# GEMM2's matmuls placed one by one inside the products of GEMM1, for ten of the 24 of a pair

## The chip, the cores and the metric

The kernel runs on one core of one Trainium2 chip. The metric is the device time of the program in microseconds (us), as the median of several runs. A profiled execution of the same program gives the trace that is read below.

## What is computed

Eight batches with eight heads of linear attention feed a feed-forward layer of 4608 tokens, 512 channels and 2048 hidden units:

```python
q_s = exp(q - max(q, -1)); q_s /= sum(q_s, -1) + 1e-9      # over head_dim
k_s = exp(k - max(k, 2));  k_s /= sum(k_s, 2) + 1e-9       # over the sequence
kv  = einsum('bhsd,bhse->bhde', k_s, v)
x   = einsum('bhsd,bhde->bhse', q_s, kv)                   # -> (4608, 512)
h   = x @ w_in                                             # (4608, 2048)  GEMM1
g   = h * clip(h + 3, 0, 6) / 6
out = g @ w_out                                            # (4608, 512)   GEMM2
```

## The kernel before

The 4608 tokens are nine blocks of 512, numbered 0 to 8. Every large operand is held as a high and a low part in a rounded 32-bit type, and every product is three matmuls (high by high, high by low, low by high). Blocks 0 and 1 go through a plain GEMM1 with matmuls that move 512 columns. Blocks 2 to 8 use a seven-product (Strassen-like) form of GEMM1: `fast_pair(j, pair)` handles two of the 16 hidden chunks at once, so there are eight pairs a block and 56 pairs in all.

In a pair, `product(n, ps, name)` is called for n = 0 to 6. Each product is six matmuls that move 256 columns (two halves of the contraction by three part combinations) and accumulates in one of three PSUM tiles: `z` (pool `ps_a`, two buffers, shared with the attention's `pm`, `pkv` and `px`) for product 0, `y` for products 2 and 6, `x` for products 1, 3, 4 and 5 (`x` and `y` in pool `ps_h`, two buffers in all, so each pair gets the same two banks). Between the products ScalarE and VectorE combine the tiles into `first` and `second`, apply the activation (`swish`), and `split` the results into high and low parts: `one` at L545, behind product 5, and `two` at L553 and L554, which wait in the list `rest` and are issued in the next pair. At its end each product calls `fetch(1)`, one DMA on the queue of SyncE that brings a factor of weights (the product twelve calls later) into the ring slot just freed.

GEMM2 of a pair is 24 matmuls that move 512 columns, 12 for `one` and then 12 for `two`, made by the generator `work` and put in the list `pend` when the pair's products are all issued (L1028). `fill(n)` takes the next n out of `pend` and issues them. So the GEMM2 matmuls of a pair are issued during the next pair, in the gaps between products: 4, then 3 and 4, then 3 and 4, then 3 and 3. The four PSUM accumulators `po` of a block are read out by `store` when the last hidden chunk's matmuls for them are done, ScalarE for the even ones and VectorE for the odd, and a DMA writes each to the output. In the last chunk of a block the matmuls come accumulator by accumulator; in the others the four that use the low part come last.

The attention of later blocks is prepared in small steps that `half` puts in `plan`, 64 places to a block and eight to a pair; `tick(j, n)` issues the steps of place n. Some of them are DMAs (`load`, `load_k`), some GpSimd copies (`q_swap`), and four kinds use TensorE: `k_turn` (`pm`), `kv_mm` (`pkv`, 40 small matmuls), and `x_mm` (`px`).

The order on TensorE, VectorE, ScalarE and GpSimd in this part is the program's own; the order of the DMAs on SyncE's queue is left to the scheduler.

The core of the order, in the text's shorthand (256 and 512 are the columns moved), is for one pair before the change:

```text
p0 p1 | 4 x 512 | tick 0 | p2 | tick 1 | p3 | 3 x 512 | tick 2 | 4 x 512 | tick 3
p4 | 3 x 512 | tick 4 | 4 x 512 | tick 5 | p5 | 3 x 512 | tick 6 | 3 x 512 | p6 | tick 7
```

Of the kernel before, what the change touches and what calls it, by code (L numbers as in the profile page):

```python
# [31 lines left out]
def attention_moe(  # L32
# [32 lines left out]
    NB = NT // TB  # L65
    NFC = w.shape[0]
# [17 lines left out]
    def ordered(ins):  # L84
        tc.keep_in_program_order(ins)

    def mm(out, lhsT, rhs, start, stop, goes_on=False):
        ordered(
            nc.tensor.matmul(  # L89
                out, lhsT, rhs, start=start, stop=stop, skip_group_check=goes_on  # L90
            )
        )
# [27 lines left out]
    def split(hi, lo, src, engine=nc.vector):  # L120

        nc.scalar.copy(hi, src)  # L122
        engine.tensor_sub(lo, src, hi.bitcast(F32))  # L123
# [76 lines left out]
    FAST = 2  # L200
# [208 lines left out]
    def factors(j):  # L409

        if j not in spare:
            (x21, x22), (t2, t3) = ((x[:, 0:2], x[:, 2:4]) for x in x_block(j % 2))
            x11, t1, t4 = (wi[3 * (j % 2) + i] for i in range(3))
            t = [x11, x21, x22, t1, t2, t3, t4]
            spare[j] = [
                (y.rearrange("p a b -> p (a b)")).rearrange(
                    "p (e i n) -> p e i n", e=2, i=2
                )
                for y in t
            ]  # L420
        return spare[j]
# [44 lines left out]
    def fetch(count):  # L466
        for _ in range(count):
            key = next(wanted, None)
            if key is None:
                return  # L470
            j, pair, n = key
            f, h = RING[next(turn) % len(RING)]
            t = wi[f].rearrange("p a n -> p (a n)")[:, h * TB : (h + 1) * TB]
            t = t.rearrange("p (e n) -> p e n", e=2)
            nc.sync.dma_start(t.bitcast(F32), kept[pair][:, ORDER[n][0]])
            come[key] = t
# [8 lines left out]
    def fast_pair(j, pair):  # L485

        to = factors(j)
        x = ps_h.tile([P, TB], F32, name="ph", tag="ph")[:, 0:HT]
        y = ps_h.tile([P, TB], F32, name="ph", tag="ph")[:, 0:HT]
        z = ps_a.tile([P, TB], F32, name="pz", tag="pa")[:, 0:HT]  # L490
        seen = set()

        def product(n, ps, name):
            w_hi, w_lo = (come[j, pair, n][:, e] for e in (0, 1))
            f_hi, f_lo = (to[ORDER[n][1]][:, e] for e in (0, 1))
            for i in range(2):
                c = slice(i * P, (i + 1) * P)
                for k, (w, f) in enumerate(((w_hi, f_hi), (w_hi, f_lo), (w_lo, f_hi))):
                    first = name not in seen
                    seen.add(name)  # L500
                    mm(ps, w[:, c], f[:, i], first, i == 1 and k == 2, True)
            del come[j, pair, n]
            fetch(1)

        def swish(r, h):
            nc.scalar.activation(r, h, AF.Relu, bias=three, scale=1.0)  # L506
            nc.vector.scalar_tensor_tensor(r, r, 6.0, h, op0=ALU.min, op1=ALU.mult)  # L507

        first = moe.tile([P, TB], F32, name="first", tag="g_hi", bufs=3)
        second = moe.tile([P, TB], F32, name="second", tag="g_lo", bufs=3)  # L510
        places = [wi[12 + 2 * (pair % 2) + n] for n in (0, 1)]
        one, two = ((t[:, 0], t[:, 1]) for t in places)
        at = 8 * pair
        product(0, z, "z")
        product(1, x, "x")
        nc.scalar.copy(first[:, 0:HT], x)
        if rest:
            rest.pop(0)()
        fill(4)
        tick(j, at)  # L520
        if rest:
            rest.pop(0)()
        product(2, y, "y")
        nc.vector.tensor_add(first[:, 0:HT], first[:, 0:HT], z)
        tick(j, at + 1)
        product(3, x, "x")
        nc.scalar.copy(second[:, 0:HT], x)
        r = moe.tile([P, TB], F32, name="g", bufs=2)
        swish(r[:, 0:HT], first[:, 0:HT])
        fill(3)  # L530
        tick(j, at + 2)
        fill(4)
        tick(j, at + 3)
        product(4, x, "x")
        nc.scalar.copy(second[:, HT:], x)
        nc.vector.tensor_add(second[:, HT:], second[:, HT:], y)
        fill(3)
        tick(j, at + 4)
        fill(4)
        tick(j, at + 5)  # L540
        product(5, x, "x")
        swish(r[:, HT:], x)
        fill(3)
        tick(j, at + 6)
        split(*one, r)  # L545
        fill(3)
        product(6, y, "y")
        nc.vector.tensor_add(second[:, 0:HT], second[:, 0:HT], y)  # L548
        r = moe.tile([P, TB], F32, name="g", bufs=2)
        nc.scalar.activation(r, second, AF.Relu, bias=three, scale=1.0)  # L550
        tick(j, at + 7)
        nc.vector.scalar_tensor_tensor(r, r, 6.0, second, op0=ALU.min, op1=ALU.mult)  # L552
        rest.append(lambda: nc.scalar.copy(two[0], r))  # L553
        rest.append(lambda: nc.vector.tensor_sub(two[1], r, two[0].bitcast(F32)))  # L554
        return [one, two]
# [3 lines left out]
    def tick(j, n):  # L559
        for fn in plan.pop((j, n), ()):  # L560
            fn()
# [322 lines left out]
    def work(j, fs, gs):  # L884

        for f, g in zip(fs, gs):
            for n, (fn, x) in enumerate(gemm2(f, *g, acc(j))):
                yield fn, x, (j, n // 3) if f == NFC - 1 and n % 3 == 2 else None

    def run(got):  # L890
        fn, x, done = got
        fn(*x)
        if done:
            j, t = done
            store(j, t, acc(j)[t])

    def fill(n=10**6):
        while pend and n:
            got = next(pend[0], None)
            if got is None:  # L900
                pend.pop(0)
                continue
            run(got)
            n -= 1
# [82 lines left out]
    def block1():  # L987
        for p in range(NFC // 2 - 1):
            d = fast_weights(p)
            for n in (0, 1, 3, 4, 5, 7):  # L990
                at(1, 8 * (p + 1) + n, lambda d=d: next(d, None))
        d7 = fast_weights(NFC // 2 - 1)
        for n in (0, 1, 3, 4, 5, 8):
            at(2, n, lambda: next(d7, None))
        for j in range(FAST, NB):
            lead = {FAST: 3, FAST + 1: 6}.get(j, 0)
            half(j, 0, 2, lead)
            half(j, 1, 3, 32, 2 if j == FAST else 0)
        fill()
        for f in range(NFC):  # L1000
            g = gemm1(1, f)
            tick(1, 4 * f)
            tick(1, 4 * f + 1)
            g.mms()
            g.relu()
            tick(1, 4 * f + 2)
            g.times()
            g.hi()
            if f % 2 and f >= 11:
                fetch(2 if f < 15 else 12 - len(come))  # L1010
            keep = f == NFC - 1
            if not keep:
                fill(6)
            tick(1, 4 * f + 3)
            gs = g.lo()
            if not keep:
                fill(6)
            pend.append(work(1, [f], [gs]))
# [3 lines left out]
    with tc.manual_schedule(engines=ORDERED):  # L1022
        block1()
        for j in range(FAST, NB):
            for pair in range(NFC // 2):
                gs = fast_pair(j, pair)
                fill()
                pend.append(work(j, [2 * pair, 2 * pair + 1], gs))  # L1028
        while rest:
            rest.pop(0)()  # L1030
        fill()
# [60 lines left out]
```

## Time and profile before

| | |
|---|---|
| median of 3 runs | 865.53 us (865.02 to 866.68) |
| the profiled execution | 865.39 us, of which the span of the instructions is 863.3 us |
| TensorE matmuls busy | 840.3 us, 97% of the span, 5380 instructions |
| weight loads busy (TensorE) | 735.7 us, 85% |
| VectorE busy | 625.1 us, 72% |
| ScalarE busy | 444.1 us, 51% |
| GpSimd busy | 70.7 us, 8% |
| granted TensorE clock | 0.998 of full |

Busy times are shares of the span. A matmul's own record lasts from its start to the modelled end of its pipeline, so records of successive matmuls overlap; the pace is read from start to start. In the rows PE is TensorE's matmuls, PEld its weight loads (each matmul has one, and it runs beside the matmul before it), DVE VectorE, ACT ScalarE, POOL GpSimd, SP SyncE.

### The profile page before, as it was taken

How to read it: one execution, taken by the hardware profiler on the slowest of the kernel's cores; microseconds unless marked ns; L12 is line 12 of the kernel's file. 1: busy time of each engine (PE TensorE's matmuls, PEld its weight loads, DVE VectorE, ACT ScalarE, POOL GpSimd, SP SyncE). 2: the span in 40 equal slices, each digit the busy share in tenths (PEclk: the TensorE clock that was granted, in tenths of full speed). 3: DMA queues.
4: the chain of work that ended last, by engine and by line, in shares of the span. 5: the costliest groups of instructions: out<-in, count | busy, mean ns of one | idle time of the engine just before them, and what ended most of it. 6: DMA issues, size and time to landing. Idle time of an engine off the chain costs nothing.

```text
span 863.3 us, 15152 instructions
## 1 busy us (share of the span) xinstructions
PE 840.3 (97%) x5380; PEld 735.7 (85%) x5380; DVE 625.1 (72%) x1275; ACT 444.1 (51%) x897; POOL 70.7 (8%) x244
## 2 busy tenths in 40 slices
PE   4799999999999999999999999999999999999998
PEld 3587888888889898989898989999898998989996
DVE  6998995989877776777776777676767676664333
ACT  6898773454544454544545445444444544453333
POOL 4000000101020101010000101010101010100000
PEclk9999999999999999999999999999999999999999
DMA  9778542537887668767776777676865666557541
GB/s 368 270 304 273 170 130 75 185 117 226 275 270 257 216 214 259 223 203 231 249 237 199 245 240 251 185 243 201 272 184 167 192 216 195 171 163 226 173 134 49
DMA packets 97114, 182.56 MB, mean 211 GB/s; under 512 B 9744, under 2 KB 24080, under 8 KB 94992
## 3 DMA queue, kind: packets, MB, share of 16 engines
q1 hardware_dynamic: 96192, 180.03, 65.0%
q10 hardware_dynamic: 576, 1.05, 0.4%
q0 software_dynamic: 272, 0.52, 0.3%
q8 instruction: 43, 0.70, 0.3%
q14 instruction: 31, 0.25, 0.1%
HBM read 156.93 MB, written 24.12 MB: 210 GB/s over the span
## 4 chain that ended last, share of the span: by engine, by line
PE 90%; DVE 4%; ACT 2%; DMA 2%; issue 1%; SPq 0%; POOL 0%; ACTq 0%; POOLq 0%; DVEq 0%
PE po L89 44%; PE ph L89 36%; PE pz L89 5%; PE px L89 3%; PE pkv L89 2%; DMA kq<-in_q_dram 1%; DMA w<-v 1%; DVE v L162 1%; ACT raw L168 1%; DVE w L188 0%; DMA raw<-in_w_dram 0%; DVE v L152 0%; DVE v L156 0%; PE pm L95 0%; ACT qt L297 0%
## 5 line engine op out<-in xcount | busy, mean ns | idle before, releaser
L89 PE MATMUL po<-w,w 128*128 128x512 f32 x1008 | 263.3, 395 | 0.0
L89 PEld LDWEIGHTS po<-w,w 128*128 128x128 f32 x1008 | 177.1, 189 | 29.0
L89 PE MATMUL ph<-w,w 128*128 128x256 f32 x1008 | 147.5, 282 | 0.0
L89 PEld LDWEIGHTS ph<-w,w 128*128 128x128 f32 x1008 | 139.7, 191 | 9.1
L89 PE MATMUL ph<-x_lo,w 128*128 128x256 f32 (+1 forms) x800 | 144.8, 301 | 0.4 <-DVE x_lo L123 0.3
L89 PE MATMUL ph<-x_hi,w 128*128 128x256 f32 (+1 forms) x592 | 135.5, 333 | 2.8 <-DVE x_lo L387 2.8
L89 PEld LDWEIGHTS ph<-x_lo,w 128*128 128x128 f32 x800 | 113.7, 189 | 11.7 <-DVE x_lo L123 0.5
L89 PEld LDWEIGHTS ph<-x_hi,w 128*128 128x128 f32 x592 | 96.1, 190 | 18.8 <-DVE x_lo L387 3.6
L621 POOL COPY swap<-qm 32x16 f32<-32x16 f32 x224 | 58.7, 262 | 626.3 <-DVE qm L615 592.3
L89 PE MATMUL po<-w 128*128 128x512 f32 x336 | 88.4, 395 | 0.1
L550 ACT ACTIVATE g<-second,three 128x512 f32<-128x512 f32 x56 | 40.7, 726 | 68.6 <-DVE second L548 67.5
L89 PEld LDWEIGHTS po<-w 128*128 128x128 f32 x336 | 58.9, 189 | 10.3 <-ACT w L553 0.5
L89 PE MATMUL po<-w,g_hi 128*128 128x512 f32 x256 | 67.6, 396 | 0.0
L123 DVE TENSOR_TENSOR w<-g,w 128x512 fp32r<-128x512 f32 x56 | 38.8, 693 | 30.7 <-ACT w L122 29.4
L507 DVE SCALAR_TENSOR_TENSOR g<-g,ph 128x256 f32<-128x256 f32 x56 | 23.5, 420 | 45.2 <-ACT g L506 44.9
L89 PEld LDWEIGHTS po<-w,g_hi 128*128 128x128 f32 x256 | 47.1, 188 | 10.1 <-issue 0.7
L552 DVE SCALAR_TENSOR_TENSOR g<-g,second 128x512 f32<-128x512 f32 x56 | 38.7, 691 | 22.9 <-ACT g L550 22.9
L553 ACT CAST w<-g 128x512 fp32r<-128x512 f32 x56 | 34.9, 623 | 31.7 <-DVE g L552 31.7
L506 ACT ACTIVATE g<-ph,three 128x256 f32<-128x256 f32 x56 | 26.4, 472 | 45.4 <-PE ph L89 45.4
L89 PE MATMUL pz<-x_hi,w 128*128 128x256 f32 x336 | 49.5, 283 | 0.0
L554 DVE TENSOR_TENSOR w<-g,w 128x512 fp32r<-128x512 f32 x56 | 38.8, 692 | 13.9 <-ACT w L553 12.1
L507 DVE SCALAR_TENSOR_TENSOR g<-g,first 128x256 f32<-128x256 f32 x56 | 23.7, 423 | 34.6 <-ACT g L506 34.6
(133 smaller groups left out, 1195.0 us busy)
## 6 DMA issues: line engine op xcount, KB each, us to landing
w<-wf SPq DMA_DIRECT2D x392, 256.0 KB, 3.1
raw<-in_w_dram SPq DMA_DIRECT2D x16, 1024.0 KB, 11.1
out_dram<-ob SPq DMA_DIRECT2D x36, 256.0 KB, 3.4
vt<-in_v_dram SPq DMA_DIRECT2D x28, 325.0 KB, 5.5
wf<-w SPq DMA_DIRECT2D x16, 512.0 KB, 3.8
kt<-in_kT_dram SPq DMA_DIRECT2D x28, 288.0 KB, 3.2
ke<-in_k_dram SPq DMA_DIRECT2D x24, 320.0 KB, 4.3
qt<-in_qf_dram SPq DMA_DIRECT2D x28, 256.0 KB, 3.7
```

What stands on the lines that cost most here:

```text
L89: nc.tensor.matmul(out, lhsT, rhs, start=start, stop=stop, skip_group_check=goes_on)
L123: engine.tensor_sub(lo, src, hi.bitcast(F32))
L162: nc.vector.scalar_tensor_tensor(vu, raw(1), 0xC0000000, vu, op0=ALU.bitwise_and, op1=ALU.bitwise_or)
L168: nc.scalar.activation(low, low, AF.Copy, scale=2.0**-29)
L506: nc.scalar.activation(r, h, AF.Relu, bias=three, scale=1.0)
L507: nc.vector.scalar_tensor_tensor(r, r, 6.0, h, op0=ALU.min, op1=ALU.mult)
L550: nc.scalar.activation(r, second, AF.Relu, bias=three, scale=1.0)
L552: nc.vector.scalar_tensor_tensor(r, r, 6.0, second, op0=ALU.min, op1=ALU.mult)
L553: rest.append(lambda: nc.scalar.copy(two[0], r))
L554: rest.append(lambda: nc.vector.tensor_sub(two[1], r, two[0].bitcast(F32)))
L621: nc.gpsimd.tensor_copy(swaps[hp][r : r + QD], qms[hp][o : o + QD])
```

## The change

Five of the 24 GEMM2 matmuls of a pair go one at a time behind each of the first five matmuls of product 0, and five more in the same way inside product 2. The other 14 go in two runs of seven, between products 3 and 4 and between 4 and 5. There are none between 1 and 2 or between 5 and 6 any more. Since product 0 of a pair comes before that, the five in it are the last five of the pair before the previous one: five stay in `pend` when a pair ends. In the first pair of block 2 and the last pair of block 8 product 0 takes none; so after the last pair 10 older matmuls are left to issue ahead of that pair's own 24.

All eight ticks move: tick 0 is now inside product 0, behind its third matmul, tick 1 is behind product 1, tick 2 behind product 2, and ticks 3 to 6 stand where 4 and 3 matmuls of 512 columns alternate in the other order. The `fill()` that drained `pend` at a pair's end is gone.

```text
p0 with 5 x 512 (tick 0 inside) | p1 | tick 1 | p2 with 5 x 512 | tick 2 | p3 | 4 x 512 | tick 3
3 x 512 | tick 4 | p4 | 4 x 512 | tick 5 | 3 x 512 | tick 6 | p5 | p6 | tick 7
```

```diff
-        def product(n, ps, name):
+        def product(n, ps, name, among=0, at=None):
...
                     mm(ps, w[:, c], f[:, i], first, i == 1 and k == 2, True)
+                    if 3 * i + k < among:
+                        fill(1)
+                    if at is not None and 3 * i + k == 2:
+                        tick(j, at)
...
-        product(0, z, "z")
+        product(0, z, "z", 0 if (j, pair) in ((FAST, 0), (NB - 1, NFC // 2 - 1)) else 5, at)
         product(1, x, "x")
         nc.scalar.copy(first[:, 0:HT], x)
         if rest:
             rest.pop(0)()
-        fill(4)
-        tick(j, at)
+        tick(j, at + 1)
         if rest:
             rest.pop(0)()
-        product(2, y, "y")
+        product(2, y, "y", 5)
         nc.vector.tensor_add(first[:, 0:HT], first[:, 0:HT], z)
-        tick(j, at + 1)
+        tick(j, at + 2)
         product(3, x, "x")
         nc.scalar.copy(second[:, 0:HT], x)
         r = moe.tile([P, TB], F32, name="g", bufs=2)
         swish(r[:, 0:HT], first[:, 0:HT])
-        fill(3)
-        tick(j, at + 2)
         fill(4)
         tick(j, at + 3)
+        fill(3)
+        tick(j, at + 4)
         product(4, x, "x")
         nc.scalar.copy(second[:, HT:], x)
         nc.vector.tensor_add(second[:, HT:], second[:, HT:], y)
-        fill(3)
-        tick(j, at + 4)
         fill(4)
         tick(j, at + 5)
+        fill(3)
+        tick(j, at + 6)
         product(5, x, "x")
         swish(r[:, HT:], x)
-        fill(3)
-        tick(j, at + 6)
         split(*one, r)
-        fill(3)
         product(6, y, "y")
         nc.vector.tensor_add(second[:, 0:HT], second[:, 0:HT], y)
...
             for pair in range(NFC // 2):
                 gs = fast_pair(j, pair)
-                fill()
                 pend.append(work(j, [2 * pair, 2 * pair + 1], gs))
```

## The prediction

> **What bounds the kernel.** I read the page's busy times and its chain of waits first, then the stage that the change touches in stretches, then one pair of it in the order of time.
>
> ```profile
> span 863.3 us, 15152 instructions
> PE 840.3 (97%) x5380; PEld 735.7 (85%) x5380; DVE 625.1 (72%) x1275; ACT 444.1 (51%) x897; POOL 70.7 (8%) x244
> ...
> PE 90%; DVE 4%; ACT 2%; DMA 2%; issue 1%; SPq 0%; POOL 0%; ACTq 0%; POOLq 0%; DVEq 0%
> ```
>
> The chain that ended last is 90% TensorE. In stretches (start and end, length, PE's busy time and instructions, granted clock, DMA share, GB/s), from the first product of block 2 to the last product of block 8, and then the tail:
>
> ```profile
> 224.78:853.40 628.62, 628.26 (x4249) 1.00 0.68 212
> 853.40:863.33 9.93, 6.20 (x26) 0.99 0.27 106
> ```
>
> TensorE leaves 0.36 us of 628.62 uncovered, at clock 1.00. So no engine or transfer holds this stage as a whole; it lasts as long as its matmuls follow each other, and the change can win only in their pace, at waits inside it, or in the tail. One pair of block 8, which has no attention steps, in the order of time (start, length of the group's records, tile, columns moved, count):
>
> ```profile
> 830.21 1.55 PE L89 MATMUL po<-w,w 128*128 128x512 f32 x6
> 831.60 0.88 PE L89 MATMUL ph<-w,w 128*128 128x256 f32 x6
> 832.31 0.88 PE L89 MATMUL pz<-x_hi,w 128*128 128x256 f32 x6
> 833.03 0.88 PE L89 MATMUL ph<-w,w 128*128 128x256 f32 x6
> 833.75 1.09 PE L89 MATMUL po<-w,w 128*128 128x512 f32 x4
> 834.68 1.59 PE L89 MATMUL ph<-x_lo,w 128*128 128x256 f32 x12
> 836.10 1.78 PE L89 MATMUL po<-w,w 128*128 128x512 f32 x7
> 837.72 0.88 PE L89 MATMUL ph<-w,w 128*128 128x256 f32 x6
> 838.43 1.78 PE L89 MATMUL po<-w,w 128*128 128x512 f32 x7
> 840.04 0.88 PE L89 MATMUL ph<-x_hi,w 128*128 128x256 f32 x6
> 840.76 1.32 PE L89 MATMUL po<-w,w 128*128 128x512 f32 x5
> ```
>
> From start to start: the 24 of 512 columns take 1.39 + 0.93 + 1.62 + 1.61 = 5.55 us, the 42 of 256 take 2.15 + 1.42 + 0.71 + 0.72 = 5.00, the pair 10.55. In the middle of a long run a 256 takes 120 ns (832.31 to 833.03 is six). In block 1, where only 512s follow each other, the chain of waits gives their undisturbed pace, 2.72 / 12 = 227 ns:
>
> ```profile
> 204.12 2.72 PE ph L89 x12
> ```
>
> So the pair's 512s pay 5.55 - 24 x 0.2267 = 0.11 us above that. Where it sits shows in single durations, grouped by shape in slits of time (the last number before the idle column is the mean ns): at 837.72 (last 512 of a run, first 256 behind it), 833.76 (last 256s of a run, first 512 behind them) and 833.99 (that first and the second 512).
>
> ```profile
> L89 PE MATMUL po<-w,w 128*128 128x512 f32 x1 | 0.4, 389 | 0.0
> L89 PE MATMUL ph<-w,w 128*128 128x256 f32 x1 | 0.3, 278 | 0.0
> ```
>
> ```profile
> L89 PE MATMUL ph<-w,w 128*128 128x256 f32 x2 | 0.4, 283 | 0.0
> L89 PE MATMUL po<-w,w 128*128 128x512 f32 x1 | 0.4, 396 | 0.0
> ```
>
> ```profile
> L89 PE MATMUL po<-w,w 128*128 128x512 f32 x2 | 0.6, 397 | 0.0
> ```
>
> A 256 behind a 512 is 278 - 283 = 5 ns shorter than its followers, and half of the locked 512 is 113 ns against 120, so I take 114 ns for it, 6 below the run. I read this as its weight load: behind a 512 it has been hidden, behind another 256 it ends a little too late. The first 512 behind a 256 pays 396 - 389 = 7 ns, the next 2 x 397 - 396 - 389 = 9 ns, and by the end of a run nothing.
>
> **The change part by part.**
>
> *Ten single 512s.* No instruction is added or removed; 5 + 5 of the 24 change places. A pair has had four runs of 256s, so four cheap first ones. Now the runs are 13, four singles, 8, four singles, 7 and 6, twelve in all: 8 more at 6 ns, -48 ns. On the other side the two runs of seven cost 1.62 + 1.61 - 14 x 0.2267 = 0.056 us above the locked pace, and the ten singles, each behind a 256, 7 ns: 0.070. Together 0.126 against 0.11 before, +16 ns. Net -32 ns a pair. The trace has no 512 between two 256s, so both ends: at best a single is free on both sides (the 512 at 227, the 256 at 114), 10 x 7 = 70 ns better than that; at worst the 9 ns which a second 512 pays is paid by the 256 that stands in its place, 90 ns worse. I take the values in between since a lone 512 has exactly the neighbours whose rows stand above: a 256 before it (396) and behind it a 256 that follows a 512 (278). 54 pairs have all ten, two have five: 55 x 32 ns = -1.8 us.
>
> A rule speaks against this. The Trainium skill, page "TensorE: Matmul & The Clock Gate", section "LDWEIGHTS (loading the stationary operand)", gives a load of 128 columns as 128 / 1.2, 107 ns, and its section "Back-to-back issue gap" gives 262 cycles at 2.4 GHz, 109 ns, for a 256-column matmul: the load would fit under each 256 already, and a 512 in between would hide nothing. By that this term would be 0, not -1.8 us. The trace has 120 and not 109 ns in the run.
>
> *The tail.* After product 6 of the last pair come 24 of 512 columns:
>
> ```profile
> 853.40 6.28 PE L89 MATMUL po<-w 128*128 128x512 f32 x24
> 856.38 0.69 DVE L554 TENSOR_TENSOR w<-g,w 128x512 fp32r<-128x512 f32 x1 [0.69 <-ACT w L553]
> 856.40 0.30 PEld L89 LDWEIGHTS po<-w 128*128 128x128 f32 x2 [0.51 <-ACT w L553]
> 857.12 2.14 PEld L89 LDWEIGHTS po<-w 128*128 128x128 f32 x10 [0.43 <-DVE w L554]
> ```
>
> From the first start to the last they take 6.28 - 0.39 = 5.89 us, where 23 locked ones take 5.21: 0.68 too long, 0.03 of it the usual start of a run, the rest waits for the high and the low part of `two`. With the change product 6 stands right behind product 5 and 10 older 512s (2.3 us) come first. Product 5 ended at 851.30 (853.40 less product 6 and the six 512s). Counted from there the matmuls of `two` then begin at 0.72 + 2.3 + 2.7 = 5.7 us and need the low part 0.45 later. The high part was ready at 856.4, which is 5.1, the low part at 856.38 + 0.69, which is 5.77, and the chain to them hangs on product 5 (below, bank `y`). No wait is left, with 0.4 us to spare: -0.65 us. If that cover were short, up to the same 0.65 would come back.
>
> *The first pair of block 2.* Product 2 waits there for the factor T3:
>
> ```profile
> 227.14 0.92 PE L89 MATMUL ph<-x_lo,w 128*128 128x256 f32 x4
> 228.40 1.21 PE L89 MATMUL ph<-x_lo,w 128*128 128x256 f32 x8 [0.34 <-DVE x_lo L123]
> ```
>
> T3 comes when it did, and product 2 now gets there 0.93 us earlier, without four 512s ahead of it; but four singles run before its fifth matmul, which is the one that waits for the low part. The same 512s are done by 228.4: 0, at most 0.2 either way.
>
> *Bank `y`.* Product 6 no longer has six 512s ahead of it, so the sum that frees `y` for the next product 2 has less time. In block 8 (product 5 ends at 840.76):
>
> ```profile
> 842.58 0.69 DVE L123 TENSOR_TENSOR w<-g,w 128x512 fp32r<-128x512 f32 x1 [0.69 <-ACT w L122]
> 843.19 0.42 DVE L548 TENSOR_TENSOR second<-second,ph 128x256 f32<-128x256 f32 x1
> ```
>
> It ends 2.85 us after product 5, held by the low part of `one` ahead of it on VectorE, not by product 6. The next product 2 begins 0.72 + (0.72 + 5 x 0.233) + 0.71 = 3.3 us after product 5 (before: 4.47, from 830.21 to 834.68). The cover is 0.45 us; a VectorE later than that stops TensorE for the difference. Pairs with attention steps can be later, by the rows
>
> ```profile
> 438.78 1.55 PE L89 MATMUL po<-w,w 128*128 128x512 f32 x6
> 442.05 0.42 DVE L548 TENSOR_TENSOR second<-second,ph 128x256 f32<-128x256 f32 x1
> ```
>
> that is 3.7 us after product 5, but behind that pair six matmuls of `px` now stand ahead of product 2, which move as many columns as three 512s (by the locked pace an estimated 0.7 us). I cost it at 0.
>
> *The ticks.* All eight move by some 1.3 us or less against TensorE. VectorE's part of a tick now often comes ahead of a sum that waits for TensorE, which fills idle time. `kv_mm` and the first `x_mm` keep 256s on both sides; `k_turn` and the second `x_mm` pass from between 512s to between a 512 and a 256:
>
> ```profile
> 424.28 0.86 PE L89 MATMUL po<-w,w 128*128 128x512 f32 x3
> ...
> 426.01 0.88 PE L89 MATMUL ph<-x_hi,w 128*128 128x256 f32 x6
> ```
>
> ```profile
> 433.31 0.98 PE L89 MATMUL ph<-x_lo,w 128*128 128x256 f32 x6
> 434.12 1.09 PE L89 MATMUL po<-w,w 128*128 128x512 f32 x4
> ```
>
> With `pm` in it a run of seven takes 1.73 us, so it costs 1.73 - 1.62 = 0.11 us; six 256s behind `pkv` cost 0.81 - 0.71 = 0.10, so the neighbour matters by 0.01: 0, with 0.3 for 40 such places.
>
> *Queues and banks.* SyncE still gets one fetch a product, 12 products ahead (by the pair above some 18 us), against 3.1, and for a tick's load 3.2,
>
> ```profile
> w<-wf SPq DMA_DIRECT2D x392, 256.0 KB, 3.1
> kt<-in_kT_dram SPq DMA_DIRECT2D x28, 288.0 KB, 3.2
> ```
>
> us to land, and a tick's loads are read seven ticks or more later, each over 1 us. GpSimd's four copies of a `q_swap` have one tick or more before VectorE reads them; the shortest, from tick 3 to tick 4, now has three 512s in it (0.7 us) instead of those and a product, and a late copy would hold VectorE first. The stores of accumulators 2 and 3 move to product 0 of a block's second pair; their banks are next written some 3 us later, in and behind product 2, against one read-out of 512 columns on ScalarE or VectorE. All 0.
>
> Sum against the profiled execution's own 865.39 us: -1.8 - 0.65 gives 863.0. The median of the runs is 865.53, 0.14 above it, which I do not carry.
>
> **The rivals.**
>
> *Nothing to hide.* Singles cost what their kind costs on average now, and only the tail is won: 865.39 - 0.65 = 864.7. For it: the change's own term is 32 ns of 10.55 us, and the 256s behind the run of four in the pair above go at 1.42 / 12 = 118 ns, so they do not simply swing between 114 and 120. Against it: the 278 and the 396. The Trainium skill's load rule, cited above, gives this time.
>
> *Free on both sides.* With time to spare on every load the singles fall to 227 and 114: 55 x 70 ns more, 863.0 - 3.9 = 859.1. For it: the last 512 of a run has 389. Against: that takes some five 512s to come about.
>
> *The wait is handed on* (slower). After a disturbed 512 the next matmul pays 9 ns whatever its kind, so the 256 costs 123: 863.0 + 550 x 9 ns = 868.0. For it: the second 512's excess cannot be its load, which had a whole 512 to hide under. Against: it fades along the run. It makes the kernel slower from 7.5 ns a single on (867.1).
>
> **How the numbers follow.** Chances: forecast 0.38, nothing to hide 0.28, free 0.16, handed on 0.14, a late `y` or another new wait 0.04. About 0.2% (1.7 us) is what a measurement of this kernel can tell from no change; 863.0 is 2.4 below 865.39, and a quarter of its chance falls within 1.7. Faster: 0.16 + 0.29 = 0.45; same: 0.09 + 0.28 = 0.37; slower 0.18. The forecast's own range is 862.0 to 864.3 (0.3 for ticks, 0.2 for block 2, 0.65 for the tail, 2 ns on each single). The range for 8 in 10 runs from 859.5 to 867.3: it leaves out the handed-on case and a late bank (0.18) and little of the free one.
>
> **What would show it.** In the profile after: a 512 in product 0 or 2 of about 396 ns and the 256 behind it of about 278; a pair of block 8 of 10.52 us; no wait of PE's loads for L553 and L554 behind the last product; no new idle of PE ahead of product 2. Wrong it is if single 256s show 285 or more, if a pair takes 10.6, or if the waits name L548.

## The result, and the profile after

The kernel after the change takes 874.13 us (median of 6 runs, 871.89 to 876.24); the kernel before, on the same chip, 866.11 us (6 runs, 864.77 to 867.91). The ratio is 1.0096, 95% interval 1.0079 to 1.0114: about 1% slower, where 863.0 was forecast and 867.3 was the end of the range.

The profiled execution took 876.14 us. Its page (span; busy time and share of each engine; the chain of waits):

```profile
span 874.0 us, 15156 instructions
PE 848.4 (97%) x5380; PEld 737.4 (84%) x5380; DVE 627.3 (72%) x1275; ACT 444.7 (51%) x897; POOL 74.5 (9%) x244
...
PE 83%; DVE 7%; ACT 2%; DMA 2%; issue 1%; POOL 0%; ACTq 0%; POOLq 0%; DVEq 0%
```

The share of VectorE in the chain rose from 4% to 7%, though its busy time is nearly the same (627.3 against 625.1): it is waited for more often, not busier. In stretches (start and end, length; busy time and instructions of PE, PEld, DVE, ACT and POOL in turn; granted clock, DMA share, GB/s), from the first product of block 2 to the last product of block 8, and the tail:

```profile
226.32:862.51 636.19, 632.68 (x4239) 564.48 (x4238) 425.03 (x923) 297.68 (x625) 52.56 (x192) 1.00 0.68 209
862.51:874.00 11.49, 7.90 (x36) 6.20 (x34) 4.20 (x7) 3.16 (x5) 0.00 (x0) 0.95 0.24 91
```

The first stretch is 636.19 us with ten matmuls fewer (4239 for 4249), where it was 628.62, and TensorE is uncovered for 3.51 us instead of 0.36. The clock is 1.00 as before. The start of block 2 is not compared: in the profiles of all the kernels below it lies anywhere from 222.2 to 227.6 us, ahead of the pairs that were edited (only z1_runs and z2_lead8 also move one step of block 1, by one place). I therefore call *net* the time from the first product of block 2 to the end of the span, against the same of before. It is +9.18 us for the change: +7.57 up to the last product and +1.61 in the tail, to the end of the last instruction at 874.05; the tail has ten more matmuls of 512 columns (2.27 us).

TensorE's waits, by what it waited for (total us, times, longest), among those at least 0.2 us long:

```profile
PE ph L89 <- DVE second L539: 1.9, 5, 0.4
...
PE ph L89 <- DVE second L548: 0.6, 1, 0.6
...
PE px L89 <- DVE v L723: 0.3, 1, 0.3
...
PE ph L89 <- ACT second L538: 0.2, 1, 0.2
```

None of these stood in the same list of before. L548 is the sum `second += y` behind product 6, the name that the prediction gave as a sign that it is wrong. The last pair of block 8 shows it:

```profile
851.54 0.88 PE L89 MATMUL ph<-w,w 128*128 128x256 f32 x6
...
853.36 0.69 DVE L123 TENSOR_TENSOR w<-g,w 128x512 fp32r<-128x512 f32 x1 [0.69 <-ACT w L122]
853.97 0.41 DVE L548 TENSOR_TENSOR second<-second,ph 128x256 f32<-128x256 f32 x1
854.43 0.39 PE L89 MATMUL ph<-x_lo,w 128*128 128x256 f32 x1 [0.57 <-DVE second L548]
```

Product 6 starts at 851.54 and is through 0.72 us later. The sum that reads it starts at 853.97, since VectorE has the low part of `one` (L123) ahead of it, and that waits for ScalarE's cast. Product 2 of the new pair (854.43) needs the bank which the sum frees, and stands still.

A larger loss is in pair 1 of blocks 3 to 6. Pair 1 of block 4 (its product 5 starts at 431.79):

```profile
430.65 1.08 POOL L621 COPY swap<-qm 32x16 f32<-32x16 f32 x4 [9.52 <-DVE qm L615]
430.95 0.35 ACT L538 COPY second<-ph 128x256 f32<-128x256 f32 x1
431.76 0.17 DVE L624 TENSOR_TENSOR qm<-qm,swap 128x16 f32<-128x16 f32 x1 [0.78 <-POOL swap L621]
431.97 0.69 DVE L625 TENSOR_TENSOR qt<-qt,qm 128x512 f32<-128x512 f32 x1
432.58 0.41 DVE L539 TENSOR_TENSOR second<-second,ph 128x256 f32<-128x256 f32 x1
433.05 0.98 PE L89 MATMUL ph<-w,w 128*128 128x256 f32 x6 [0.38 <-DVE second L539]
```

GpSimd's swap keeps VectorE waiting for 0.78 us, a step of the attention follows, and only then comes L539, the sum that frees `y` for product 6. Product 6 starts 1.26 us behind product 5 (431.79 to 433.05) instead of 0.72. And in pair 0 product 2 waits for its factor T3 (pair 0 of block 4):

```profile
413.24 0.41 DVE L548 TENSOR_TENSOR second<-second,ph 128x256 f32<-128x256 f32 x1
413.74 0.72 ACT L550 ACTIVATE g<-second,three 128x512 f32<-128x512 f32 x1 [1.15 <-DVE second L548]
414.37 0.60 ACT L122 CAST x_lo<-v 128x512 fp32r<-128x512 f32 x1
415.01 0.69 DVE L123 TENSOR_TENSOR x_lo<-v,x_lo 128x512 fp32r<-128x512 f32 x1 [1.36 <-ACT x_lo L122]
415.75 0.19 PEld L89 LDWEIGHTS ph<-x_lo,w 128*128 128x128 f32 x1 [0.36 <-DVE x_lo L123]
```

The late sum releases the relu (L550), ScalarE's cast for T3 (L122) stands behind that relu, and T3's low part (L123) behind the cast.

From the first matmul of a pair to that of the next, against the same pair of before (us; the first pair of block 2 and the last of block 8 hold five matmuls of 512 columns fewer, 1.13 us):

| block | pair 0 | 1 | 2 | 3 | 4 | 5 | 6 | 7 |
|---|---|---|---|---|---|---|---|---|
| 2 | -0.69 | +0.12 | +0.27 | +0.01 | +0.56 | +0.70 | 0.00 | +0.13 |
| 4 | +0.22 | +0.67 | 0.00 | +0.10 | +0.29 | +0.07 | 0.00 | +0.11 |
| 8 | +0.21 | +0.04 | +0.04 | +0.04 | +0.04 | +0.04 | +0.04 | -0.30 |

So the loss is +0.04 us in an undisturbed pair, and waits of 0.1 to 0.8 us at certain places.

### The profile page after: what moved, and what is told of

Its sections match the earlier page's. It is cut to its first block, busy times and chain, and to the rows that moved or that the text cites. A ratio compares the mean times of both kernels' runs of the same rounds, so it can differ in the third digit from the quotient of the medians.

```text
span 874.0 us, 15156 instructions
## 1 busy us (share of the span) xinstructions
PE 848.4 (97%) x5380; PEld 737.4 (84%) x5380; DVE 627.3 (72%) x1275; ACT 444.7 (51%) x897; POOL 74.5 (9%) x244
## 4 chain that ended last, share of the span: by engine, by line
PE 83%; DVE 7%; ACT 2%; DMA 2%; issue 1%; POOL 0%; ACTq 0%; POOLq 0%; DVEq 0%
PE po L89 40%; PE ph L89 33%; PE pz L89 4%; PE px L89 3%; PE pkv L89 2%; DMA kt<-in_kT_dram 1%; DMA w<-v 1%; ACT w L122 1%; DVE w L123 1%; ACT g L550 1%; DVE ke L604 0%; DVE qt L625 0%; DVE w L188 0%; DVE v L162 0%; ACT g L510 0%
## 5 line engine op out<-in xcount | busy, mean ns | idle before, releaser
L89 PE MATMUL po<-w,w 128*128 128x512 f32 x1008 | 301.1, 395 | 0.0
L89 PEld LDWEIGHTS po<-w,w 128*128 128x128 f32 x1008 | 184.1, 189 | 33.6
L89 PE MATMUL ph<-x_lo,w 128*128 128x256 f32 (+1 forms) x800 | 187.5, 302 | 1.1 <-DVE second L548 0.6
L89 PEld LDWEIGHTS ph<-x_lo,w 128*128 128x128 f32 x800 | 132.0, 189 | 12.2 <-DVE x_lo L123 2.6
L89 PEld LDWEIGHTS ph<-w,w 128*128 128x128 f32 x1008 | 133.9, 190 | 9.1 <-DVE second L539 3.0
L89 PE MATMUL po<-w 128*128 128x512 f32 x336 | 97.7, 394 | 0.0
L89 PE MATMUL pz<-x_hi,w 128*128 128x256 f32 x336 | 93.1, 282 | 0.0
L550 ACT ACTIVATE g<-second,three 128x512 f32<-128x512 f32 x56 | 40.5, 723 | 64.6 <-DVE second L548 63.5
L123 DVE TENSOR_TENSOR w<-g,w 128x512 fp32r<-128x512 f32 x56 | 38.8, 692 | 38.4 <-ACT w L122 38.4
L89 PEld LDWEIGHTS pz<-x_hi,w 128*128 128x128 f32 x336 | 63.1, 190 | 0.1
L552 DVE SCALAR_TENSOR_TENSOR g<-g,second 128x512 f32<-128x512 f32 x56 | 38.6, 690 | 23.0 <-ACT g L550 23.0
L553 ACT CAST w<-g 128x512 fp32r<-128x512 f32 x56 | 34.8, 622 | 30.5 <-DVE g L552 30.4
L122 ACT CAST w<-g 128x512 fp32r<-128x512 f32 x56 | 34.7, 620 | 27.3 <-DVE g L511 26.8
```

What stands on the lines that cost most here:

```text
L89: nc.tensor.matmul(out, lhsT, rhs, start=start, stop=stop, skip_group_check=goes_on)
```

## The experiments

*The theory* that stands at the end: the singles cost a little, and the rest comes from VectorE. With product 6 directly behind product 5, the sum L548 still has to wait for the low part of `one`, so it and all that follows it in VectorE's queue come later against the products of the next pair. *The rivals*: the singles themselves, a price for each passage from one width to the other, and the moved ticks. "Net" is read from the profile, the ratio from runs of both kernels on one chip; the chips differ from row to row, so medians of different rows are not to be compared.

| kernel | median us | ratio to before (95%) | net us |
|---|---|---|---|
| the change | 874.13 | 1.0096 (1.0079, 1.0114) | +9.18 |
| x1_runs5 | 875.11 | 1.0101 (1.0079, 1.0123) | +7.71 |
| x2_tick4 | 873.74 | 1.0088 (1.0063, 1.0113) | +6.62 |
| x3_three | 870.34 | 1.0053 (1.0033, 1.0073) | +4.73 |
| y1_both | 871.98 | 1.0072 (1.0052, 1.0092) | +5.62 |
| x4_hold | 864.35 | 0.9983 (0.9966, 1.0000) | -0.71 |
| y2_four | 868.02 | 1.0017 (0.9998, 1.0035) | +1.63 |
| y3_thirteen | 868.30 | 1.0032 (1.0012, 1.0053) | +2.72 |
| y5_sumfirst | 866.33 | 1.0011 (0.9992, 1.0030) | +1.00 |
| w1_near | 887.09 | 1.0240 (1.0220, 1.0261) | +20.32 |
| s1_runs5sum | 866.11 | 0.9992 (0.9979, 1.0004) | +0.06 |
| z1_runs | 865.92 | 1.0004 (0.9991, 1.0018) | -0.14 |
| z2_lead8 | 867.04 | 1.0020 (1.0005, 1.0035) | +3.58 |

### x1_runs5: the change without singles

```diff
-        product(0, z, "z", 0 if (j, pair) in (...) else 5, at)
+        product(0, z, "z", 0, at)
+        fill(0 if (j, pair) in (...) else 5)
...
-        product(2, y, "y", 5)
+        fill(5)
+        product(2, y, "y")
```

> The changed kernel with no single 512s: the five of product 0 go in one run between products 0 and 1, the five of product 2 in one run between products 1 and 2; all steps of ScalarE and VectorE and all ticks stay as changed. Theory 'two costs': the 9.2 us lost behind block 1 are some 2.2 us from the singles themselves (54 pairs by 0.04) and some 7 us from new waits on VectorE's order. Then pairs without attention go back from 10.59 to 10.55, the waits of product 2 (for T3 and, in the last pair, for y: 1.1 and 0.7 us) go since product 2 starts 1.2 us later in its pair, and the 0.63 us wait of product 6 in the second pair of blocks 3 to 6 stays: 869 to 871 us. Rival 'the interleaving is all of it': pairs with attention also fall back to the time before, 865 to 866 us.

An undisturbed pair of block 8 goes from +0.04 to +0.01 us, and the last pair loses its wait for `y`, since the five now stand ahead of product 2 (-0.30 to -1.11, that is 0.81 us). Pair 1 of blocks 3 to 6 keeps its +0.67. The ratio isn't better than the change's (875.11 us, where 869 to 871 was expected), though the intervals are wider than the 1.5 us by which the profiles differ. The wait for T3, which was expected to go, went in blocks 7 and 8 (pair 0 at -0.01), but pair 0 of blocks 3, 5 and 6 keeps +0.17 to +0.19. The singles are not where the 9 us went.

### x2_tick4, x3_three, y1_both: a tick back, a run back

```diff
 # x2_tick4, to the change
         fill(3)
-        tick(j, at + 4)
         product(4, x, "x")
         nc.scalar.copy(second[:, HT:], x)
         nc.vector.tensor_add(second[:, HT:], second[:, HT:], y)
+        tick(j, at + 4)
```

```diff
 # x3_three, to the change; y1_both has both edits
         tick(j, at + 5)
-        fill(3)
         tick(j, at + 6)
         product(5, x, "x")
...
+        fill(3)
         product(6, y, "y")
```

> The changed kernel with tick 4 moved back behind product 4 and the sum of second and y (where it stood before), all else as changed. Theory 'the sum behind tick 4': VectorE's steps of tick 4 stand ahead of the sum that frees y for product 6, and it waits there 0.54 us in the second pair of blocks 3 to 6 and the sixth of block 2. Then these waits go: 3 us off, 870.5 to 872 us, the other pairs as they are. Rival 'interleaving': no change, 874 us.

> The changed kernel with the run of three between products 4 and 5 moved to between products 5 and 6; singles as changed. Theory 'product 6 too near to product 5': the chain of VectorE that frees y and makes T3's low part hangs on product 5, so with nothing between 5 and 6 the next product 2 comes 1.2 us too early for it. Then the 0.73 us wait in the last pair, the 0.2 us waits in the first pair of blocks 3 to 8 and the 0.1 us waits of px go: 1.9 to 2.5 us off, 872 us; the 0.54 us waits of product 6 stay. Rival 'interleaving': no change, 874 us.

> The changed kernel with both mends at once: tick 4 behind product 4 and its sum, and the run of three between products 5 and 6 (singles kept). Theory 'two costs': hardly a wait of TensorE is left, pairs without attention stay at 10.59 us (0.04 above before, the price of ten singles), pairs with attention come to within 0.1 of that: the stage 2 to 3 us above before for the same work, the tail 0.65 below: 867 to 868 us. Rival 'other waits take their place' (tick 4 behind product 4 made the pairs with the second x_mm 0.2 us longer when it was moved alone): 869 us or more.

With tick 4 behind the sum L539, pair 1 falls from +0.67 to +0.01 and the waits for L539 are gone from the list. But pairs 3 and 7 rise to +0.29 to +0.41, and the ratio hardly moves: 873.74 us, where 870.5 to 872 was expected. With three 512s between products 5 and 6, pair 0 falls from +0.22 to -0.08 and the last pair from -0.30 to -0.99, as VectorE then has 0.7 us more for what hangs behind product 5; pair 1 stays at +0.59. The first pair of block 2 loses more there, +1.14 instead of +0.44 for the same work (its wait is read further below). The two together were expected to add up, at 867 to 868 us, and did not (871.98): pair 1 is at +0.29, pairs 3 and 7 at +0.27 to +0.39. So the ticks' places decide where TensorE waits, not whether. What both edits leave as it was, beside the singles, is the order of the sum and the low part on VectorE; y5_sumfirst tries that.

### x4_hold: the tail alone

```diff
 # to the kernel before
+        last = (j, pair) == (NB - 1, NFC // 2 - 1)
-        fill(4)
+        fill(0 if last else 4)
...
-        fill(3)
+        fill(0 if last else 3)
...
-        fill(3)
+        fill(0 if last else 3)
         product(6, y, "y")
...
-                fill()
```

> The kernel before with only the tail of the change: in the last pair of block 8 the run of four and the last six 512s are left out, so that 10 older 512s stand ahead of that pair's own 24 at the end; no singles, ticks as before. Theory: the waits for the two parts of the last result go (0.65 us), 864.8 to 865.3 us beside 865.5 to 866.1 of before, and the last 34 follow each other at 227 ns. Rival: other waits in the last pair eat it (product 2 comes 1.4 us sooner there): no difference.

Every pair is within 0.01 us of before; the last is 2.31 shorter, the tail 1.61 longer: -0.71 us net, and the ratio agrees (864.35 us, where 864.8 to 865.3 was expected). The ten held matmuls cover both waits for `two`: the 34 of the tail follow each other at 227 ns.

### y2_four, y3_thirteen: singles in the kernel before

```diff
 # y2_four: the run of four goes singly inside product 1
-        product(1, x, "x")
+        product(1, x, "x", 4)
...
-        fill(4)
```

y3_thirteen has that and three singles each in products 4, 5 and 6, with runs of 4, 4 and 3 left.

> The kernel before, with the run of four between products 1 and 2 given as four singles inside product 1 instead; every step of the other engines and every tick where it was. Measures singles by themselves. Theory 'a price for each passage between the two sizes': one passage with a run of four cost 8 ns and four single ones about 7 each, so +0.02 us in each of the 56 pairs and no new wait, 1 us in all. Rival 'singles save': -0.02 us in each pair, as the prediction's 6 and 7 ns would have it. Rival 'singles are the whole loss': several us.

> The kernel before with 13 singles a pair: four in product 1 as in the kernel with four, three each in products 4, 5 and 6, taken from the runs ahead of them (which become 4, 4 and 3); the steps of the other engines in their order before. Theory 'a price for each passage': two runs of four, one of three and 13 singles make 0.07 us a pair above before, 4 us in all, 869 us, without new waits of product 6 or 2. Rival 'singles save or cost nothing': 865 us.

Four singles cost +0.02 us a pair, as expected; that they save anything falls. Thirteen cost 0.00 us in an undisturbed pair where +0.07 had been expected, so a fixed price for each passage between widths falls too. In block 2 both lose more, +0.88 and +2.37 us of a net of +1.63 and +2.72: there product 5 waits for the copy by which ScalarE reads product 4's bank (`second`, L536), for 0.3 us in y2_four and 0.9 in y3_thirteen. In y2_four that copy stands on ScalarE behind a cast of the attention (L649, 268.36 to 268.98), which had waited 1.71 us for VectorE. y2_four took no matmul from ahead of product 5, so lost cover there can't be its reason; what made VectorE late in it isn't shown.

### y5_sumfirst: the sum ahead of the low part

```diff
 # to the change; `y` is read before the low part is made
         swish(r[:, HT:], x)
-        split(*one, r)
+        nc.scalar.copy(one[0], r)
         product(6, y, "y")
         nc.vector.tensor_add(second[:, 0:HT], second[:, 0:HT], y)
+        nc.vector.tensor_sub(one[1], r, one[0].bitcast(F32))
```

> The changed kernel with one swap on VectorE: the sum of second and y behind product 6 goes ahead of the low part of one (which stood ahead of it). TensorE's order is as changed. Theory 'the chain hangs on product 5 by that low part': y comes free 1.2 us earlier, so the last pair's 0.73 us wait for y and the 0.2 us waits for T3 in the first pairs of blocks 3 to 8 and the 0.1 us waits of px go, 2 us or more off; the 0.54 us waits of product 6 for the other sum stay: 871 to 872 us. Rival 'VectorE has too much work there whatever the order': no change, 874 us.

This exchange of two instructions on one engine takes the ratio from 1.0096 to 1.0011. I had expected 871 to 872, because I thought that the waits for L539 were the tick's own. They are gone too. Of its waits at least 0.2 us long, two are in this stage:

```profile
PE px L89 <- DVE v L724: 0.2, 1, 0.2
PE ph L89 <- ACT second L538: 0.2, 1, 0.2
```

The same places in its pair 1 of block 4, in the order of time:

```profile
427.71 1.08 POOL L622 COPY swap<-qm 32x16 f32<-32x16 f32 x4 [9.22 <-DVE qm L616]
...
429.65 0.41 DVE L539 TENSOR_TENSOR second<-second,ph 128x256 f32<-128x256 f32 x1
...
430.10 0.88 PE L89 MATMUL ph<-x_hi,w 128*128 128x256 f32 x6
430.81 0.88 PE L89 MATMUL ph<-w,w 128*128 128x256 f32 x6
...
432.30 0.42 DVE L548 TENSOR_TENSOR second<-second,ph 128x256 f32<-128x256 f32 x1
432.42 0.62 ACT L546 CAST w<-g 128x512 fp32r<-128x512 f32 x1 [0.49 <-DVE g L511]
...
433.07 0.69 DVE L549 TENSOR_TENSOR w<-g,w 128x512 fp32r<-128x512 f32 x1 [0.35 <-ACT w L546]
```

L548 now starts 1.49 us after product 6 starts (430.81), and the low part (L549) behind it; in the last pair of the change it was 2.43 (851.54 to 853.97), and in this same pair of the change 3.56 (433.05 to 436.61). GpSimd's swap starts 2.4 us ahead of product 5 (430.10), where in the change it was 1.1 (430.65 to 431.79), and L539 is through before product 6 comes. Pair 0 is at -0.08, pair 1 at +0.03, pairs 3 and 7 at or below +0.03. So from block 3 on one late sum on VectorE, at the end of a pair, made the waits of all of the next pair. In block 2 pairs 0 and 4 keep what they lost (+0.44 for the same work, and +0.51): these have other causes.

### w1_near: product 6 directly behind product 5, and nothing else

```diff
 # to the kernel before
+        fill(6)
         product(5, x, "x")
         swish(r[:, HT:], x)
-        fill(3)
         tick(j, at + 6)
         split(*one, r)
-        fill(3)
         product(6, y, "y")
```

> The kernel before with one thing of the change: product 6 comes directly behind product 5. The six matmuls of 512 columns that stood between them go ahead of product 5 (a run of 13 between products 4 and 5, tick 6 behind product 5); no singles, all other places and ticks as before. Theory (the loss hangs on what VectorE does behind product 5): VectorE's low part of `one` and the sum that frees `y` come 1.4 us later relative to the next pair's products, so product 2 waits some 0.2 us in pair 0 of blocks 3 to 8 and there are new waits for `second` in attention pairs; pairs without attention steps change by less than 0.02 us. Sum of all pairs +2 to +6 us, ratio 1.002 to 1.007. Rival (the moved ticks or the singles are what the loss needs): every pair within 0.05 us of before, ratio 0.999 to 1.001.

The direction is that of the theory, the size far above it: +20.3 us net instead of +2 to +6. An undisturbed pair loses 0.25 us here, pair 0 1.35. What was missed shows in an undisturbed pair of block 8:

```profile
833.68 0.41 DVE L547 TENSOR_TENSOR second<-second,ph 128x256 f32<-128x256 f32 x1
834.19 0.72 ACT L549 ACTIVATE g<-second,three 128x512 f32<-128x512 f32 x1 [1.15 <-DVE second L547]
834.35 1.85 PE L89 MATMUL ph<-x_lo,w 128*128 128x256 f32 x12
834.82 0.35 ACT L516 COPY first<-ph 128x256 f32<-128x256 f32 x1
```

and in its waits:

```profile
PE ph L89 <- ACT x_lo L122: 3.6, 6, 0.6
PE ph L89 <- ACT first L516: 2.6, 5, 0.5
PE ph L89 <- DVE x_lo L123: 2.4, 7, 0.3
PE po L89 <- ACT w L122: 1.0, 1, 1.0
```

The late sum (here L547) releases ScalarE's relu (L549) late. The copy of product 1 (L516) queues behind it, and product 3 needs the bank which the copy reads: the twelve matmuls of products 2 and 3 take 1.85 us where 1.59 stood before. T3's high and low part hang on the same queues. The tail is 1.37 us longer too (11.30 for 9.93). With nothing between products 5 and 6 of the last pair, its 24 matmuls start 1.11 us behind product 6, when the high part of `one` is there (the last row), and 0.26 us more is lost among them, where `two` is waited for. In the change and in x1_runs5, which have five 512s about product 0 and five ahead of or in product 2, an undisturbed pair shows nothing of this (+0.04 and +0.01). So in pairs without attention steps these ten, singly or not, hid nearly all of the loss that the late sum makes; w1_near has the late sum without that cover.

### s1_runs5sum: singles against runs where there are no waits

The edit is that of x1_runs5, made to y5_sumfirst.

> The change with the sum on VectorE ahead of the low part of `one` (which took away nearly all waits) and with the ten singles set as two runs of five, one behind product 0 and one behind product 1. What the singles alone cost, by the pairs without attention steps: theory (a single costs 2 to 4 ns more than its kind does in a run) -0.03 us a pair, +0.01 to before, so the sum of all pairs falls by 1.7 us and the ratio goes from 1.001 to 0.999. Rival (the price of the singles was a property of the kernel with waits): no change, +0.04 a pair, ratio 1.001.

An undisturbed pair is +0.01 us as in x1_runs5, 0.03 below the one with singles, and the net falls from +1.00 to +0.06 us. That is 0.94 and not the expected 1.7: outside block 2 and pair 0, pairs with attention steps were at -0.02 to +0.04 with singles already. The ratio goes from 1.0011 to 0.9992 (0.9979, 1.0004); the two intervals overlap, so the 0.94 rests on the two profiles.

### z1_runs, z2_lead8: towards a version that is faster

```diff
 # z1_runs, to y5_sumfirst
-        product(0, z, "z", 0 if ... else 5, at)
+        product(0, z, "z", 0, at)
+        fill(0 if early_ or late_ else 4)
...
-        product(2, y, "y", 5)
+        fill(4 if early_ else 0)
+        product(2, y, "y")
+        n = 4 if early_ or late_ else 5
-        fill(4)
+        fill(n)
...
-            (31, t_both),
+            (30, t_both),
```

```diff
 # z2_lead8, to z1_runs
-            lead = {FAST: 3, FAST + 1: 6}.get(j, 0)
+            lead = {FAST: 3, FAST + 1: 8}.get(j, 0)
```

All four runs between products 3 and 5 are `fill(n)`, with the ticks where they were. z1_runs also issues the attention step `t_both` one place earlier (30 instead of 31), which no run tries alone.

> The change with the sum on VectorE put ahead of the low part of `one`, and without singles: 4 older matmuls of 512 columns between products 0 and 1, ten between 3 and 4, ten between 4 and 5, so that three runs stand where before had five; in the last pair 12 older ones stay for the tail. Theory (the waits are gone with the sum moved ahead, the singles cost 0.04 us a pair, fewer runs save 0.01 to 0.03): plain pairs -0.02 us, tail -0.65 to -0.7, sum -1 to -2.5 us, ratio 0.997 to 0.999. Rival (other waits in pairs with attention steps take the place, as they did when two parts were put together before): sum of the pairs above +1 us, ratio 1.001 to 1.004.

> The version with three runs (4 + 10 + 10) and the sum ahead, with one number more: the attention steps that block 2 does for block 3 start 8 places after the block's start instead of 6, so that they meet the same places of a pair as in the other blocks. Theory (the 2.0 us of new waits in block 2, 0.39 in its pair 2 and 1.62 in its pair 4, come from that offset alone): block 2 -0.9 us to before instead of +1.25, sum with the tail -2.2 us, ratio 0.997 to 0.999. Rival (two sets of steps then overlap in block 2's second half and wait for each other): block 2 +0.5 us or more, ratio 1.000 or above.

In z1_runs the undisturbed pairs are at -0.03 to -0.01 us and every pair from block 3 on is faster or at most 0.04 slower. The tail is -0.66 (12 more matmuls, 2.72 us, for +2.06). But block 2 has two new waits, pair 2 with +0.39 and pair 4 with +1.62:

```profile
PE px L89 <- DVE v L728: 1.4, 1, 1.4
...
PE pm L95 <- DVE km L599: 0.2, 1, 0.2
```

So the net is -0.14 us and the ratio 1.0004: no difference. Setting block 2's steps two places later, to take these waits away, made new ones (block 2 from +1.25 to +4.96 us). That is the rival's time; its reason, that two sets of steps wait for each other, was not followed in the trace. No version that I ran beats the kernel before by more than the measurement can tell, apart from x4_hold, at the edge with 0.9983.

## Why the prediction was wrong

**The tail** was right: forecast -0.65 us, measured -0.66 in the change (+1.61 for ten matmuls worth 2.27), where the 34 matmuls follow each other without a wait, and -0.71 net with that part alone, in x4_hold.

**The ten singles** were mis-sized, with the wrong sign. In block 8 of the change, singles in product 0, in the order of time:

```profile
831.21 0.40 PE L89 MATMUL po<-w,w 128*128 128x512 f32 x1
831.44 0.28 PE L89 MATMUL pz<-x_hi,w 128*128 128x256 f32 x1
831.56 0.40 PE L89 MATMUL po<-w,w 128*128 128x512 f32 x1
...
832.86 0.28 PE L89 MATMUL pz<-x_hi,w 128*128 128x256 f32 x1
832.98 0.88 PE L89 MATMUL ph<-w,w 128*128 128x256 f32 x6
```

Five 512s and the five 256s behind them take 832.98 - 831.21 = 1.77 us, 354 ns for the two, where 234 + 114 = 348 was forecast. Read singly from start to start, the 512s take 232 to 241 ns (236 on average) and the 256s 114 to 120 (118). So a 256 behind a single 512 keeps only 2 of the 6 ns that it has behind a run, and the 512 pays 9 instead of 7. The records' own lengths (396 to 403 ns and 277 to 284) were nearly those I named as the proof. They couldn't prove it: the price was in the starts, and a difference of single lengths, 5 ns, was not known to 2. Of the three signs named for being wrong only the waits for L548 came; 284 ns for a 256 and 10.59 us for a pair stayed just inside. Per pair it came to +0.04 us instead of -0.032, and against runs at the same places, in kernels without waits, to 0.94 us in all (y5_sumfirst less s1_runs5sum), where -1.8 against before was forecast. The Trainium skill's rule for a weight load, page "TensorE: Matmul & The Clock Gate", section "LDWEIGHTS (loading the stationary operand)", which I set against this term and by which it would be 0, was nearer than my reading, though it doesn't give the loss.

**The first pair of block 2** (forecast 0, at most 0.2): -0.69 with 1.13 us less work, so +0.44, and the same in y5_sumfirst and s1_runs5sum. The wait for T3 that was costed came out right: the fifth matmul of product 2 starts 3.62 us into the pair (229.94 less 226.32), as before (228.40 less 224.78). What was missed is product 5 of the change:

```profile
234.58 0.62 ACT L445 CAST w<-s 128x512 fp32r<-128x512 f32 x1 [1.28 <-DVE s L443]
235.10 0.36 ACT L538 COPY second<-ph 128x256 f32<-128x256 f32 x1
235.52 0.98 PE L89 MATMUL ph<-x_hi,w 128*128 128x256 f32 x6 [0.20 <-ACT second L538]
```

L538 is ScalarE's copy of product 4, which frees the bank for product 5. It stands behind a cast of tick 4 (L445) that waits for VectorE. In x3_three, with three 512s fewer ahead of product 5, this wait is 0.9 us. In x2_tick4 and y1_both, where tick 4 stands behind L538 and L539, the pair is at -1.14: the loss hangs on tick 4 ahead of them.

**Bank `y`** is the step that failed, together with **the ticks**, both costed at 0. The number in it was right where I took it from: in block 8 the sum ends 2.84 us after product 5 (851.54 to 854.38), with 2.85 forecast, and undisturbed pairs don't wait for it. Three things were not followed from there.

1. In the last pair product 0 takes no singles, as I wrote myself. Product 2 then comes 1.16 us sooner than the 3.3 that I used, and the cover of 0.45 us becomes a wait; moving five 512s ahead of product 2 (x1_runs5) took 0.81 us off that pair.
2. I asked only when the sum frees `y`, and not what stands behind it. Before, with 4.47 us from product 5 to the next product 2, the lateness cost nothing. With 3.3 us, 1.2 less, the relu L550 and the step L552 come that much later in the new pair, and with them ScalarE's and VectorE's queues: T3 in pair 0, the maximum and the swaps of the attention, then L539.
3. For the ticks I wrote that VectorE's part "fills idle time". It does so only while VectorE runs ahead of TensorE. Once late, a step that waits for GpSimd (0.78 us in the rows of pair 1) holds the next sum, and that holds TensorE. y5_sumfirst keeps the ticks' new places and has hardly a wait from block 3 on, so there the 0 for the ticks failed only through the late sum; by itself it failed in the first pair of block 2.

The Trainium skill, page "Perfetto Trace Analysis", section "Tensor Engine Instruction (MATMUL, LD_WEIGHTS)", says that VectorE, ScalarE and GpSimd take their queues strictly first in, first out. The trace agrees: L539's last operand, a copy by ScalarE, was there by 431.30 (430.95 + 0.35 in the change), and it started at 432.58, behind L625. By that rule, the order in which a late step and a sum are issued was worth a row of the prediction.

What the sum becomes, net of the start: the exchange of two instructions on VectorE takes +9.18 to +1.00, so 8.2 us were the late sum, by the profiles (by the ratios, 1.0096 to 1.0011, some 7 of 866); the singles are 0.9, the tail -0.66, the first pair of block 2 +0.44 (these three in y5_sumfirst's +1.00). The rest is small and of both signs: pair 4 of block 2 (+0.49 in s1_runs5sum, its cause open), and pair 0 of the other six blocks, about 0.1 us faster each there.

**The rivals.** "The wait is handed on" had the right side, for the most part by luck: it said 868.0 us by 9 ns a single, and a single cost 6 ns more than forecast (354 for 348), some 1 us of the 8 that were lost. "Nothing to hide" was nearer in the singles' own cost, and fell with the bank. "Free on both sides", 227 + 114 = 341 ns, is out. "A late `y` or another new wait" had a chance of 0.04, without a time worked out; it was the case that came.

## What to carry to other kernels

When an edit brings two producers closer together, don't ask only whether the next consumer still finds its buffer free. Write down the queue of each engine that reads them, from the late instruction on, and compare each entry's start with the point at which TensorE will want it; a slack of 0.4 us in pairs without other work says nothing of pairs with it.

When moving a tick or a run removes a wait and another appears elsewhere, look for one lateness that all of them share. Here it was two neighbouring instructions in the wrong order on VectorE, and exchanging them was worth 8 us, where moving one tick or one run was worth 2.6 or 4.5.

## What the runs showed of the hardware

The order of widths hardly matters to TensorE here, and not by a fixed amount for each passage: ten singles cost 0.03 us a pair against runs of five (0.04 against 0.01), four cost 0.02, and thirteen among short runs 0.00. The same matmul of 512 columns takes 232 to 236 ns in three of the five places inside a product and 241 in the other two, for which no run here gives a reason.
